# The first MoE's output projection taken out of the attention steps and made a phase of seven block products

## Chip, cores and metric

One NeuronCore of a Trainium2 chip. The metric is the device time of one execution in microseconds; a few runs are shown by their median. The engines are TensorE (PE, matrix products), VectorE (DVE), ScalarE (ACT), GpSimd (POOL) and SyncE (SP, which issues most DMA transfers).

## Reference

Attention with a causal mask and a decay bias, then two MoE layers that use all their weights for each token:

```python
scores = q @ k.T / 8 + min(bias(cumsum(max(s, 0))), 0)      # 4 batches, 8 heads, 576 tokens, 64 wide
x  = softmax(causal(scores)) @ v                            # 2304 tokens x 512
h  = max(max(x @ w1, x @ w2), x @ w3)                       # 512 -> 768
x2 = h @ w_out                                              # 768 -> 512, "first MoE's output projection"
h2 = (x2 @ w_a) * (x2 @ w_b)                                # 512 -> 1536
out = h2 @ w_out2                                           # 1536 -> 512
```

## The kernel before

**Products in two parts.** Each operand of a matrix product is kept as a rounded part "h" and a remainder "l" (a rounding on ACT or POOL, `rnd`, and a subtraction on DVE, `sub` or `hilo` at lines 937 to 939). A product takes three matmuls: h by h, h by l, l by h. The weights come as 64-bit numbers and are first made 32-bit (`conv_w`, line 234, and `to_f32`, line 915).

**Attention and first MoE.** The work is cut into eight steps: four batches, each with the first 256 tokens (R = 0) and the other 320 (R = 1). In a step four pairs of heads go through scores (PE), softmax (DVE, ACT, DVE, POOL), transposes (PE, copied by ACT) and the product with v (`f_pv`, line 520), whose result is split into Xh and Xl. The first three steps are "plain" (scores without the split). `moe1_units` (line 589) makes the first MoE's units of a step: 18 gate units of 12 matmuls (`gate`, line 594; ACT copies the first product into hf, DVE takes the two maxima, ACT rounds the result into hh and DVE writes hl), and four output units of 18 matmuls (`outp`, line 622; ACT copies the result into xo and its queue stores it to the DRAM tensor x2T, x transposed). The units of a step may start when all four pairs of that step are done. A list with positions (lines 805 to 874) spreads them over the next step's attention, with the attention at a higher priority; a list scheduler then fixes each engine's order, so that a unit's matmuls fill what the attention leaves free. The units that are left at the end run alone (lines 1092 to 1096), and between them pieces that prepare the second MoE are put in by hand, each after a "mark", the eviction of some unit.

**Second MoE.** Tokens are taken in three blocks of 768, and each 512-deep product of a block is made with seven products of half-size blocks instead of eight: `a_side` (line 942) and `b_side` (line 960) form seven operands from the four quarters with four sums each, and `Unit.prod` (line 1148) runs the products in the order 1, 2, 6, 5, 7, 4, 3 into three PSUM banks X, Y and Z. Products 6, 7 and 4 add onto bank X, which ACT copies after products 1, 6 and 7; product 3 adds onto Z. `x2_load` (line 1027, SP's queue) fetches x2T for a block, `x2_split` (line 1034) makes its operands. `w2_pieces` (line 990) prepares one of 12 column groups of both gate weights. `gates` (line 1179) is one unit of 7 x 6 matmuls of 384 columns. The results go to hT in DRAM, and a last phase of 256-column products makes the output.

**Memory.** Tiles lie in pools on a left and a right stack. A pool that is allocated with `reuse_waits="tile"` over released ones makes each new tile wait for the old tiles under it.

Of the kernel before, what the change touches and what calls it, by code (L numbers as in the profile page):

```python
# [29 lines left out]
def kernel(  # L30
# [18 lines left out]
    nc = tc.nc  # L49
# [56 lines left out]
    ap_ = tc.alloc_tile_pool(name="attn", bufs=1, side="right")  # L106

# [27 lines left out]
    x2T = dram.tile([DM, NT], F32, name="x2T")  # L135
# [117 lines left out]
    w1o = []  # L253
    w1_keys = [("g", g, m) for m in range(MF) for g in range(3)]
    w1_keys += [("o", m) for m in range(MF)]
    w1_t = {}

# [5 lines left out]
    NPRE = 4  # L263
    for p_, n0, n1 in zip(w1p, (0, 6, 11, 18), (6, 11, 18, NPRE - MF)):
        w1_tiles(p_, w1_keys[n0:n1])
# [30 lines left out]


# [7 lines left out]
    def load_pair(b, p, R):  # L305
# [9 lines left out]
        if b == 0 and p >= 2 and R == 0 and plain:  # L315
            t = mp.tile([P, MF * N1], F32, tag="hh" if bp == 2 else "hl", bufs=1, name="kqv")
# [260 lines left out]
    w1_pend = list(w1_keys)  # L577
# [11 lines left out]
    def moe1_units(R, b, X):  # L589
# [4 lines left out]
        def gate(m, g):  # L594
# [13 lines left out]
            if g == 0:  # L608
                st["h"] = mp.tile([P, N1], F32, tag="mt", bufs=2, name="hf")
                st["A"] = nc.scalar.copy(st["h"][:, :n], ps[:, :n])  # L610
            else:
                hf = st["h"][:, :n]
                st["V"] = nc.vector.tensor_tensor(hf, ps[:, :n], hf, op=ALU.max)  # L613
                mark(st["A"], st["V"])
            if g == 2:
                if m == 0:
                    st["hh"] = mp.tile([P, MF, N1], F32R, tag="hh", bufs=1, name="hh")
                    st["hl"] = mp.tile([P, MF, N1], F32R, tag="hl", bufs=1, name="hl")
                rnd("A", st["hh"][:, m, :n], hf)
                sub("V", st["hl"][:, m, :n], hf, f(st["hh"][:, m, :n]))  # L620

        def outp(c):
            ps = ps_m.tile([P, 512], F32, tag="m", name="o")
            hh, hl = st["hh"], st["hl"]
            mm = []
            for m in range(MF):
                key = ("o", m)
                if key not in w1h:
                    w1_need(key)
                mm += [(w1h[key], hh, m), (w1h[key], hl, m), (w1l[key], hh, m)]  # L630
            for i, (w, x, m) in enumerate(mm):
                nc.tensor.matmul(  # L632
                    ps[:, :n], w[:, c, :], x[:, m, :n],
                    start=(i == 0), stop=(i == len(mm) - 1),
                )
            xo = mp.tile([P, N1], F32, tag="mt", bufs=2, name="xo")
            mark(nc.scalar.copy(xo[:, :n], ps[:, :n]))  # L637
            nc.scalar.dma_start(x2T[c * P : (c + 1) * P, col : col + n], xo[:, :n])
# [6 lines left out]
        for c in range(KC):  # L645
            units.append((18 * w, lambda c=c: outp(c)))
# [217 lines left out]
    for j in range(MF):  # L864
        stream.append((W1 + (W2 - W1) * j / MF, 200, w_next))
# [9 lines left out]
    moe = [(1, m_next) for _ in range(len(todo))]  # L875
    ap_.release()

    TB = 384
    NSB = NT // (2 * TB)
    KH = KC // 2
    OPS = (1, 2, 6, 5, 7, 4, 3)
    sides = ("right", "left")

    rA = tc.alloc_tile_pool(name="rA", bufs=1, side="right", reuse_waits="tile")
    rA2 = tc.alloc_tile_pool(name="rA2", bufs=1, side="right", reuse_waits="tile")
    xr = {0: tc.alloc_tile_pool(name="xr0", bufs=1, side="right", reuse_waits="tile")}  # L900
    wpool = {0: rA}
    rawp = [rA2]
    nraw = [0]

    def load_raw(src):

        pool = rawp[nraw[0] % len(rawp)]
        nraw[0] += 1
        raw = pool.tile([P, WC, 2], I32, tag="raw", bufs=1, name="wraw")
        rv = raw.rearrange("p c t -> p (c t)")  # L910
        if not wide:
            return raw, nc.sync.dma_start(rv[:, :WC].bitcast(F32), src)
# [665 lines left out]
```

## Time and profile before

| | |
|---|---|
| runs, median (lowest, highest) | 906.07 us (906.06, 908.05), 3 runs |
| span of the profiled execution | 903.9 us, first to last instruction; the median is 2.2 us more |
| instructions | 17169 |
| TensorE clock granted | full in all 40 slices |
| busy share PE, DVE, ACT, POOL | 99%, 65%, 42%, 25% |
| HBM read, written | 77.29 MB, 23.94 MB |

The span starts with the attention; the last attention products end at 448 us, the last output unit of the first MoE at 498 us, the second MoE's gates at 757 us. Durations of matmuls in the profile overlap, so the pace of a stream of matmuls is read from a stretch divided by their count, not from their mean duration.

### The profile page before, as it was taken

What the parts mean: (1) busy time and instruction counts of PE and PEld (TensorE: products, weight loads), DVE (VectorE), ACT (ScalarE), POOL (GpSimd) and SP (SyncE); (2) the same over time, 40 slices, a digit from 0 to 9 for tenths busy, and PEclk for the clock granted to TensorE, in tenths of its full rate; (3) what the DMA queues carried; (4) which work ended last, traced back from release to release, by engine and by line L of the source; (5) the groups of instructions that cost most, each with busy time, mean ns of one, the idle gap of its engine ahead of it and who ended that gap; (6) DMA issues with size and microseconds to landing.
All of it is one profiled execution on the core that took longest, in us unless ns stands there. A gap on an engine that the chain in (4) does not pass through costs nothing.

```text
span 903.9 us, 17169 instructions
## 1 busy us (share of the span) xinstructions
PE 892.1 (99%) x6296; PEld 849.5 (94%) x6296; DVE 590.9 (65%) x1401; ACT 381.3 (42%) x877; POOL 223.8 (25%) x336
## 2 busy tenths in 40 slices
PE   7999999999999999999999999999999999999998
PEld 7677899999999999999999999999999999999998
DVE  4798543556545555455379567777675868997874
ACT  3656553656536565265433332223222223433321
POOL 6553421222312223132122102111111210321211
PEclk9999999999999999999999999999999999999999
DMA  5665441213322233221143214444443244254331
GB/s 180 218 197 189 128 118 30 88 48 104 99 62 73 62 103 91 70 60 51 45 156 131 85 48 154 158 155 146 146 146 123 99 157 141 80 168 157 99 117 47
DMA packets 57228, 102.36 MB, mean 113 GB/s; under 512 B 5960, under 2 KB 40680, under 8 KB 57144
## 3 DMA queue, kind: packets, MB, share of 16 engines
q1 hardware_dynamic: 52536, 96.54, 34.0%
q10 hardware_dynamic: 4608, 4.72, 1.6%
q8 instruction: 50, 0.82, 0.4%
q14 instruction: 34, 0.28, 0.1%
HBM read 77.29 MB, written 23.94 MB: 112 GB/s over the span
## 4 chain that ended last, share of the span: by engine, by line
PE 93%; DMA 3%; DVE 1%; issue 1%; SPq 1%; ACT 1%; POOL 0%; ACTq 0%; POOLq 0%
PE g L604 25%; PE X L1125 24%; PE Z L1125 12%; PE o L632 9%; PE Y L1125 6%; PE fpv L540 5%; PE t L556 3%; DMA wraw<-in_moe_w_dram 2%; PE f L473 2%; PE s L429 2%; PE s L430 2%; PE W L1125 1%; PE ft L515 1%; PE tj L569 1%; PE sj L463 1%
## 5 line engine op out<-in xcount | busy, mean ns | idle before, releaser
L604 PE MATMUL g<-Xh,hg 128*128 128x256 f32 (+1 forms) x576 | 174.4, 304 | 0.5 <-ACT xo L637 0.5
L604 PE MATMUL g<-Xh,lg 128*128 128x256 f32 (+1 forms) x576 | 172.8, 301 | 0.0
L604 PE MATMUL g<-Xl,hg 128*128 128x256 f32 (+1 forms) x576 | 172.5, 300 | 0.0
L604 PEld LDWEIGHTS g<-Xh,hg 128*128 128x128 f32 x576 | 108.5, 189 | 4.1 <-issue 2.0
L604 PEld LDWEIGHTS g<-Xl,hg 128*128 128x128 f32 x576 | 108.8, 189 | 2.3 <-issue 0.7
L604 PEld LDWEIGHTS g<-Xh,lg 128*128 128x128 f32 x576 | 108.7, 189 | 1.0 <-issue 0.8
L1125 PE MATMUL X<-xh,wh 128*128 128x384 f32 x288 | 97.3, 338 | 0.1
L1125 PE MATMUL X<-xl,wh 128*128 128x384 f32 x288 | 96.9, 336 | 0.0
L1125 PE MATMUL X<-xh,wl 128*128 128x384 f32 x288 | 96.9, 337 | 0.0
L88 POOL TENSOR_SCALAR wh<-wval 128x256 fp32r<-128x256 f32 x84 | 41.4, 502 | 181.8 <-DVE wval L929 134.7
L1125 PE MATMUL X<-woh,slot 128*128 128x256 f32 x408 | 76.6, 281 | 0.5 <-ACT ob L1168 0.5
L422 POOL TENSOR_SCALAR P<-P,rs 128x128 f32<-128x128 f32 (+2 forms) x80 | 51.8, 653 | 98.2 <-DVE rs L417 64.3
L935 DVE TENSOR_TENSOR slot<-hraw,slot 128x768 fp32r<-128x768 f32 x60 | 60.4, 1032 | 13.8 <-POOL slot L88 11.0
L935 DVE TENSOR_TENSOR u<-Z,u 128x384 f32<-128x384 f32 x72 | 39.7, 552 | 43.2 <-ACT u L1168 33.5
L613 DVE TENSOR_TENSOR hf<-g,hf 128x256 f32<-128x256 f32 (+1 forms) x96 | 43.5, 453 | 34.0 <-PE g L604 32.4
L1125 PEld LDWEIGHTS X<-woh,slot 128*128 128x128 f32 x408 | 64.3, 189 | 0.7 <-ACT ob L1168 0.7
L405 DVE CUSTOM_DVE_ANT_0 P<-s,maskJ 128x128 f32<-128x128 f32 (+2 forms) x80 | 40.3, 516 | 26.9 <-PE s L430 13.7
L632 PE MATMUL o<-hh,lo 128*128 128x256 f32 (+1 forms) x192 | 57.8, 305 | 0.0
L632 PE MATMUL o<-hh,ho 128*128 128x256 f32 (+1 forms) x192 | 57.0, 302 | 0.3 <-ACT xo L637 0.3
L1125 PE MATMUL X<-wol,slot 128*128 128x256 f32 x204 | 56.9, 280 | 0.0
L632 PE MATMUL o<-hl,ho 128*128 128x256 f32 (+1 forms) x192 | 56.5, 299 | 0.0
L412 ACT ACTIVATE P<-P,nm 128x128 f32<-128x128 f32 (+2 forms) x80 | 46.5, 582 | 22.6 <-DVE nm L405 16.9
(168 smaller groups left out, 2255.1 us busy)
## 6 DMA issues: line engine op xcount, KB each, us to landing
hT<-u SPq DMA_DIRECT2D x72, 192.0 KB
hraw<-hT SPq DMA_DIRECT2D x36, 384.0 KB
wraw<-in_moe_w_dram SPq DMA_DIRECT2D x18, 512.0 KB
wraw<-in_moe_w_out_dram SPq DMA_DIRECT2D x18, 512.0 KB
kraw<-in_kT_dram SPq DMA_DIRECT2D x24, 288.0 KB
wraw<-in_moe_w_a_dram SPq DMA_DIRECT2D x12, 512.0 KB
wraw<-in_moe_w_b_dram SPq DMA_DIRECT2D x12, 512.0 KB
out_dram<-ob SPq DMA_DIRECT2D x18, 256.0 KB
```

The lines of the kernel that those rows point to most:

```text
L88: nc.gpsimd.tensor_scalar(o, i, scale, 1.0, op0=ALU.mult, op1=ALU.mult)
L405: nc.vector.tensor_tensor_reduce(pt[:, c0 : c0 + w], v_, m_, -scale, first, op0=ALU.add, op1=ALU.min, accum_out=nm[:, i : i + 1],)
L412: e_ = nc.scalar.activation(pt[:, c0:c1], pt[:, c0:c1], AF.Exp, bias=first, scale=-1.0, accum_out=sm[:, g : g + 1],)
L422: nc.gpsimd.tensor_scalar(pt[:, c0:c1], pt[:, c0:c1], rs[:, g : g + 1], 1.0, op0=ALU.mult, op1=ALU.mult,)
L429: nc.tensor.matmul(ps, QA1[:, qs], KB1[:, h, ksl], start=True, stop=False)
L540: e_ = nc.tensor.matmul(ps[h * D : h * D + D, c0:n], w, x, start=(t == 0), stop=(t == len(mm[h]) - 1),)
L556: nc.tensor.transpose(ps[:, j * P : j * P + P], pt[:, j * P : j * P + P], ident)
L604: nc.tensor.matmul(ps[:, :n], w[:, kk, :], x[:, kk, :], start=(i == 0), stop=(i == len(mm) - 1),)
L613: st["V"] = nc.vector.tensor_tensor(hf, ps[:, :n], hf, op=ALU.max)
L632: nc.tensor.matmul(ps[:, :n], w[:, c, :], x[:, m, :n], start=(i == 0), stop=(i == len(mm) - 1),)
L935: return {"V": nc.vector, "P": nc.gpsimd}[e].tensor_tensor(o, a, b, op=op)
L1125: nc.tensor.matmul(ps[:, :n], w, x, start=(first and i == 0), stop=(i == len(mm) - 1), skip_group_check=not first,)
```

## The change

The output units leave `moe1_units`. A step's gate result hf is no longer split; ACT's queue stores it to a DRAM tensor h1T (768 x 2304). When all gate units are done, a new phase computes the projection for the three blocks of 768 tokens with the same seven products: the two halves of the 768 rows of h and of w_out are the inner halves, two units (p = 0, 1) give the 512 output columns. One product of one unit is 9 matmuls of 384 columns. The results stay in the SBUF tile xt (two blocks at a time), from which `x2_split` makes the second MoE's operands.

The weights of the projection are only made 32-bit and kept in the tiles vo, together with the first pair of second-MoE weights, which are now loaded in steps 1 and 2 and split at positions 2.2 and 2.4 of the list (`w20_side`). Their operands for the seven products are made behind the last attention step (`wo1_side`). Block 0's operands are made there too, in three slices, with sums on DVE and roundings shared between ACT and POOL. Blocks 1 and 2 use one tile hrB in turn: roundings on ACT, subtractions on DVE, sums on POOL, in six slots (A to F) that later products reuse. `chain` fixes PE's order in this phase.

```diff
-    w1p = [tc.alloc_tile_pool(name=f"w1p{i}", bufs=1, side="left") for i in range(4)]
+    w1p = [tc.alloc_tile_pool(name=f"w1p{i}", bufs=1, side="left") for i in range(3)]
...
+    rA = tc.alloc_tile_pool(name="rA", bufs=1, side="right")
+    vo = tc.alloc_tile_pool(name="vo", bufs=1, side="right")
...
-    x2T = dram.tile([DM, NT], F32, name="x2T")
+    h1T = dram.tile([MF * P, NT], F32, name="h1T")
...
+    side_keys = [("o", m) for m in range(MF)] + [("c", 0), ("c", 1)]
...
+    def load_side(key, raw):
+
+        while len(side_v) < 2:
+            side_v.append(vo_tile(f"vo{len(side_v)}"))
+        if key[0] == "o":
+            h, k = divmod(key[1], MF // 2)
+            to_f32(raw, [(side_v[h][:, k * WC : (k + 1) * WC], slice(0, WC))])
+        else:
+            o = [t[:, KM * WC :].rearrange("r (s c) -> r s c", s=2)[:, key[1]] for t in side_v]
+            to_f32(raw, [(o[0], slice(0, 2 * P)), (o[1], slice(2 * P, 4 * P))])
...
             if g == 0:
-                st["h"] = mp.tile([P, N1], F32, tag="mt", bufs=2, name="hf")
+                st["h"] = mp.tile([P, N1], F32, tag="mt", bufs=4, name="hf")
...
             if g == 2:
-                if m == 0:
-                    st["hh"] = mp.tile([P, MF, N1], F32R, tag="hh", bufs=1, name="hh")
-                    st["hl"] = mp.tile([P, MF, N1], F32R, tag="hl", bufs=1, name="hl")
-                rnd("A", st["hh"][:, m, :n], hf)
-                sub("V", st["hl"][:, m, :n], hf, f(st["hh"][:, m, :n]))
-
-        def outp(c):
...
-            nc.scalar.dma_start(x2T[c * P : (c + 1) * P, col : col + n], xo[:, :n])
+                nc.scalar.dma_start(h1T[m * P : (m + 1) * P, col : col + n], hf)
...
-        for c in range(KC):
-            units.append((18 * w, lambda c=c: outp(c)))
...
-    for j in range(MF):
-        stream.append((W1 + (W2 - W1) * j / MF, 200, w_next))
+    ns = len(side_keys)
+    for j in range(ns):
+        stream.append((W1 + (W2 - W1) * j / ns, 200, w_next))
+    for j in range(2):
+        stream.append((W2 + 0.2 * (j + 1), 200, lambda j=j: w20_side(j)))
...
+    def h_load(sb, k0, k1, q):
 
         t0 = 2 * sb * TB
+        for n in (0, 3, 1, 2):
+            k, t = n % 2 * KM, t0 + n // 2 * TB
+            nc.sync.dma_start(q[:, n], h1v[:, k + k0 : k + k1, t : t + TB])
...
+    pieces = {
+        0: lambda: (h_fetch(0), h_fetch(1)),
+        1: lambda: h_split(0, hq[0], EN, (0,), 0, 1),
+        2: lambda: h_split(0, hq[0], EN, (1,), 0, 1),
+        3: lambda: h_fetch(2),
+        4: lambda: h_split(0, hq[1], EN, (0,), 1, 2),
+        5: lambda: h_split(0, hq[1], EN, (1,), 1, 2),
+        7: lambda: h_split(0, hq[2], EN, (0,), 2, 3),
+        8: lambda: h_split(0, hq[2], EN, (1,), 2, 3),
+    }
...
+    with tc.high_priority(300):
+        after(marks[-13], lambda: wo1_side(0, (0,)))
+        after(marks[-12], lambda: wo1_side(1, (0,)))
+        after(marks[-10], lambda: wo1_side(0, (1,)))
+        after(marks[-9], lambda: wo1_side(1, (1,)))
...
+    def oproj(p, sb):
+
+        o = xt[:, sb % 2, p]
...
+            for k in range(KM):
+                out_ += [
+                    (wh[:, k], xh[:, k]), (wh[:, k], xl[:, k]), (wl[:, k], xh[:, k]),
+                ]
...
+        return Unit(
+            TB, mms, lambda: o[:, 0], lambda: o[:, 1], lambda: o[:, 3],
+            lambda ps, t: nc.scalar.copy(o[:, 2], ps), lambda t: None,
+        )
+
+    def h_op(sb, i, n):
+        hilo(HE[i], hop[sb][0][i], hop[sb][1][i], hq[sb][:, n])
+
+    def h_sum(sb, o, a, b, op):
+        q = hq[sb]
+        tt("P", q[:, o], q[:, a], q[:, b], op)
+
+    HE = dict(zip((1, 2, 4, 6, 5, 7, 3), "AAAAAAA"))
+
+    def h_sums(sb):
+        h_sum(sb, 3, 2, 3, ALU.add)
+        h_sum(sb, 2, 0, 2, ALU.subtract)
+        h_sum(sb, 0, 3, 0, ALU.subtract)
+        h_sum(sb, 1, 1, 0, ALU.subtract)
+
+    def run_sb(sb, plan):
+        us = [oproj(p, sb) for p in range(2)]
+        for n, i in enumerate(OPS):
+            for u in us:
+                u.prod(i)
+            for fn in plan.get(i, ()):
+                fn()
+
+    SLOT = {
+        1: {1: "A", 2: "B", 4: "C", 6: "D", 5: "E", 7: "F", 3: "B"},
+        2: {1: "A", 2: "D", 4: "E", 6: "F", 5: "C", 7: "B", 3: "D"},
+    }
+    SRC = {1: 0, 2: 1, 4: 3, 6: 0, 5: 3, 7: 2, 3: 1}
...
+    def h_make(sb, i):
+        s_ = SLOT[sb][i]
+        h_tile(slots1[s_], sb, i, s_)
+        h_op(sb, i, SRC[i])
+
+    def x0_split(k, part):
+        q = [xt[:, 0, k : k + 1, n] for n in range(4)]
+        behind(lambda: x2_split(0, k, k + 1, q, EN, (part,)))
...
+    hq[1] = hq[2] = hrB.tile([P, 4, KM, TB], F32, name="hrB")
+    with tc.high_priority(300):
+        h_load(1, 0, KM, hq[1])
+    run_sb(0, {
+        1: [lambda: h_make(1, 1), lambda: h_make(1, 4)],
+        2: [lambda: h_make(1, 2), lambda: h_sums(1)],
+    })
+    hs0.release()
+    vo.release()
...
+    with tc.high_priority(100):
+        h_make(1, 6)
+        h_make(1, 5)
+        h_make(1, 7)
+        for n in (0, 3, 2):
+            h_load1(2, n)
...
+    run_sb(1, {
+        1: [lambda: h_make(2, 1), lambda: x0_split(0, 0)],
+        2: [lambda: h_make(1, 3), lambda: h_load1(2, 1), lambda: x0_split(0, 1)],
+        6: [lambda: h_make(2, 2)],
+        5: [lambda: h_make(2, 4), lambda: h_sums(2)],
+        7: [lambda: h_make(2, 6), lambda: x0_split(1, 0), lambda: more_raw(1)],
+        4: [lambda: h_make(2, 5), lambda: x0_split(1, 1)],
+        3: [lambda: h_make(2, 7)],
+    })
+    run_sb(2, {2: [lambda: h_make(2, 3)]})
...
+    with tc.high_priority(100):
+        after(hist[-4], lambda: q1[0](0, wa))
+        more_raw(1)
+        after(hist[-3], lambda: q1[0](1, wb))
+        after(hist[-2], lambda: q1[1]((0,)))
+        after(hist[-2], lambda: q1[1]((1,)))
+        after(hist[-2], lambda: xt_split(1, (0,)))
+        after(hist[-1], lambda: xt_split(1, (1,)))
```

## Rows read from the trace of the kernel before

**Rows 1.** The page: engines' busy time over the span; granted TensorE clock by slice.

```profile
PE 892.1 (99%) x6296; PEld 849.5 (94%) x6296; DVE 590.9 (65%) x1401; ACT 381.3 (42%) x877; POOL 223.8 (25%) x336
...
PEclk9999999999999999999999999999999999999999
```

**Rows 2.** PE's waits: engine, line <- releaser: us in total, times, longest.

```profile
PE f L473 <- DMA kqv<-in_kq_dram: 3.6, 1, 3.6
...
PE t L556 <- POOL F L422: 0.2, 1, 0.2
```

**Rows 3.** The page: the chain that ended last, share of the span by line.

```profile
PE g L604 25%; PE X L1125 24%; PE Z L1125 12%; PE o L632 9%; PE Y L1125 6%; PE fpv L540 5%; PE t L556 3%; DMA wraw<-in_moe_w_dram 2%; PE f L473 2%; PE s L429 2%; PE s L430 2%; PE W L1125 1%; PE ft L515 1%; PE tj L569 1%; PE sj L463 1%
```

**Rows 4.** Windows: us, each engine's busy us (instructions), granted clock, DMA share, GB/s.

```profile
core 0: us, PE busy (x) PEld busy (x) DVE busy (x) ACT busy (x) POOL busy (x), PEclk, DMA share, GB/s
45.00:100.00 55.00, 54.81 (x375) 40.71 (x375) 47.34 (x137) 31.88 (x77) 25.18 (x32) 1.00 0.57 178
90.00:120.00 30.00, 30.00 (x221) 25.00 (x217) 15.89 (x67) 18.63 (x57) 11.89 (x19) 1.00 0.41 121
186.60:300.40 113.80, 113.80 (x887) 108.29 (x886) 60.62 (x195) 62.05 (x158) 29.80 (x48) 1.00 0.28 79
457.00:487.00 30.00, 30.00 (x205) 30.00 (x205) 28.46 (x63) 12.60 (x26) 9.56 (x16) 1.00 0.51 171
560.00:757.00 197.00, 196.90 (x1131) 196.58 (x1130) 142.16 (x303) 58.97 (x114) 31.59 (x62) 1.00 0.43 142
```

**Rows 5.** The chain in order of time: start, us, what (two unbroken pieces).

```profile
101.96 1.68 PE o L632 x14
...
161.55 2.20 PE o L632 x15
```

**Rows 6.** Groups by line: out<-in xcount | busy us, mean ns | idle before.

```profile
L92 DVE TENSOR_TENSOR hl<-hf,hh 128x256 fp32r<-128x256 f32 (+1 forms) x48 | 23.9, 498 | 7.4 <-ACT hh L81 7.4
L81 ACT ACTIVATE hh<-hf 128x256 fp32r<-128x256 f32 (+1 forms) x48 | 21.2, 441 | 35.7 <-DVE hf L613 35.6
...
L637 ACT COPY xo<-o 128x256 f32<-128x256 f32 (+1 forms) x32 | 12.4, 396 | 15.1 <-PE o L632 12.4 <-DMA x2T<-xo 2.6
```

**Rows 7.** Instructions on x2T: xcount: ns min/median/max, first and last start.

```profile
L638 ACTq DMA_DIRECT2D x2T<-xo x32: 326/326/443, 108.2 to 499.0; - x32
L1032 SPq DMA_DIRECT2D xt<-x2T x16: 338/424/469, 446.0 to 502.2; - x16
```

**Rows 8.** Timeline of DVE, back to back: start us, us, what.

```profile
460.20 0.55 DVE L935 TENSOR_TENSOR xl<-xt,xh 128x384 fp32r<-128x384 f32 x1
460.67 0.55 DVE L935 TENSOR_TENSOR xt<-xt 128x384 f32<-128x384 f32 x1
461.13 0.48 DVE L613 TENSOR_TENSOR hf<-g,hf 128x320 f32<-128x320 f32 x1
...
512.45 0.95 DVE L935 TENSOR_TENSOR xl<-xt,xh 128x768 fp32r<-128x768 f32 x1
513.31 0.55 DVE L935 TENSOR_TENSOR u<-Z,u 128x384 f32<-128x384 f32 x1
```

**Rows 9.** Groups by line and shape, columns as in rows 6.

```profile
L935 DVE TENSOR_TENSOR wl<-wval,wh 128x256 fp32r<-128x256 f32 x84 | 35.4, 435 | 0.3 <-POOL wh L88 0.3
...
L81 ACT ACTIVATE xh<-xt 128x768 fp32r<-128x768 f32 x10 | 7.9, 843 | 1.1 <-DVE xt L935 1.1
...
L88 POOL TENSOR_SCALAR xh<-xt 128x384 fp32r<-128x384 f32 x6 | 4.5, 751 | 25.0 <-DVE xt L935 12.7 <-DMA xt<-x2T 12.3
...
L81 ACT ACTIVATE xh<-xt 128x384 fp32r<-128x384 f32 x8 | 4.1, 528 | 7.5 <-DMA xt<-x2T 4.0 <-DVE xt L935 3.5
...
L182 POOL TENSOR_TENSOR cl<-cs,ch 16x1152 fp32r<-16x1152 f32 x1 | 2.6, 2620 | 0.3 <-ACT ch L181 0.3
```

**Rows 10.** Timeline of POOL behind the attention.

```profile
459.36 0.52 POOL L88 TENSOR_SCALAR xh<-xt 128x384 fp32r<-128x384 f32 x1 [5.60 <-DVE xt L935]
463.63 1.76 POOL L88 TENSOR_SCALAR xh<-xt 128x384 fp32r<-128x384 f32 x1 [3.76 <-DVE xt L935]
```

**Rows 11.** DMA from 457 to 487 us in 40 slices, GB/s.

```profile
GB/s 0 266 83 0 0 0 0 0 0 0 0 109 186 377 99 221 369 381 295 287 326 348 385 309 148 229 355 393 355 93 11 0 0 0 0 0 153 333 353 358
```

More of the change, by code (lines that the diff above doesn't have):

```diff
@@ new lines, in to_f32 @@
+    def to_f32(raw, outs):
+        if not wide:
+            rv = raw.rearrange("p c t -> p (c t)")[:, :WC].bitcast(F32)
+            for o, c in outs:
+                nc.vector.tensor_copy(o, rv[:, c])
+            return
+        L = raw[:, :, 0]
+        Hw = raw[:, :, 1]
+        nc.scalar.activation(
+            f(Hw), f(Hw), AF.Prelu, scale=2.0 ** -112, alpha=-(2.0 ** 32)
+        )
+        nc.vector.tensor_scalar(L, L, 29, None, op0=ALU.logical_shift_right)
+        for o, c in outs:
+            nc.vector.scalar_tensor_tensor(
+                o.bitcast(I32), Hw[:, c], 3, L[:, c],
+                op0=ALU.logical_shift_left, op1=ALU.bitwise_or,
+            )
@@ new lines, in b_side, with w2_ops @@
+    def b_side(q, sp, part):
+        b11, b12, b21, b22 = q
+        if 0 in part:
+            sp(1, b11)
+            sp(2, b21)
+            sp(3, b22)
+            tt("V", b11, b12, b11, ALU.subtract)
+            tt("V", b12, b22, b12, ALU.subtract)
+            tt("V", b22, b22, b11, ALU.subtract)
+            tt("V", b21, b21, b22, ALU.subtract)
+        if 1 in part:
+            sp(6, b22)
+            sp(5, b11)
+            sp(7, b12)
+            sp(4, b21)
+    def w2_ops(pool, c):
+        hi, lo = {}, {}
+        for i in OPS:
+            for d, x in ((hi, "h"), (lo, "l")):
+                d[i] = pool.tile(
+                    [P, 2 * P], F32R, tag=f"w{x}{i}", bufs=1, name=f"w{x}{i}_{c % 2}"
+                )
+        wm[c] = hi, lo
+        return hi, lo
@@ new lines, with load_raw, more_raw @@
+    wpool = {0: rA}
+    rawp = [rA2]
+    nraw = [0]
+    def load_raw(src):
+        pool = rawp[nraw[0] % len(rawp)]
+        nraw[0] += 1
+        raw = pool.tile([P, WC, 2], I32, tag="raw", bufs=1, name="wraw")
+        rv = raw.rearrange("p c t -> p (c t)")
+        if not wide:
+            return raw, nc.sync.dma_start(rv[:, :WC].bitcast(F32), src)
+        return raw, nc.sync.dma_start(rv, src.bitcast(I32))
+    raws = []
+    coming = []
+    def more_raw(n):
+        for src in coming[:n]:
+            raws.append(load_raw(src))
+        del coming[:n]
+        return raws[-1][1].ins
@@ new lines, in load_w2, with x2_split, sp @@
+    def load_w2(c):
+        conv, side = w2_pieces(c)
+        for n, src in enumerate((wa, wb)):
+            conv(n, src)
+        if coming:
+            more_raw(2)
+        side((0, 1))
+    xs = {}
+    def x2_split(sb, k0, k1, q, eng, part):
+        if sb not in xs:
+            xs[sb] = {}, {}
+            for i in (1, 2, 4, 6, 5, 7, 3):
+                pool = xr1[{1: 0, 2: 0, 4: 1, 6: 1}.get(i, 2)] if sb == 1 else xr[sb]
+                for d, c in zip(xs[sb], "hl"):
+                    d[i] = pool.tile([P, KH, TB], F32R, name=f"x{c}{sb}{i}")
+        hi, lo = xs[sb]
+        es = dict(zip((1, 2, 4, 6, 5, 7, 3), eng))
+        def sp(i, src):
+            hilo(es[i], hi[i][:, k0:k1], lo[i][:, k0:k1], src)
+        a_side(q, sp, part)
@@ L1177 @@
+    strict[0] = False
+    hs1b.release()
+    hs1a.release()
+    hs1A.release()
+    hrB.release()
+    for p_ in reversed(wops):
+        p_.release()
+    rawB = lpool("rawB")
+    wpool[1] = lpool("wB")
+    xr1 = [lpool(f"xr1{n}") for n in range(3)]
+    tmpA = lpool("tmpA")
+    xr[2] = lpool("xr2")
+    wo32 = []
     hT = dram.tile([MF2 * P, NT], F32, name="hT")
@@ L1292 @@
     tmpA.release()
-    xr1b.release()
-    xr[1].release()
+    for p_ in reversed(xr1):
+        p_.release()
     wpool[1].release()
```

373 lines of the change are left out of this document (148 added, 225 removed).

## Prediction

> **What bounds the kernel now.** I read the page first: TensorE (PE) is busy for 892.1 of 903.9 us at full granted clock (2.4 GHz) in every slice, VectorE (DVE) is second with 590.9 us [rows 1]. Then PE's waits: the longest is 3.6 us, at the start, and a transpose that waited for POOL's normalised softmax is the only wait inside the attention, 0.2 us [rows 2]. So the kernel is as long as PE's instruction stream, and an edit counts by what it does to that stream or by an idle stretch that it opens. The chain of waits, followed back from the end, gives the output projection ("o L632") 9% of the span on the page [rows 3]. The windows show how near the next engine is: DVE is 86% busy in 45 to 100 us, 53% in a batch of the steady attention (186.6 to 300.4 us), 95% in the gate units behind the last attention step (457 to 487 us), and PE has no gap beside it even there [rows 4].
>
> **PE's work.** Before: four units of 18 matmuls in each of eight steps, 288 matmuls of 256 columns and 288 of 320. In unbroken pieces of the chain 14 of the first kind take 1.68 us (120 ns each), 15 of the second 2.20 us (147 ns) [rows 5]: 34.6 + 42.3 = 76.9 us. After: 3 blocks x 2 units x 7 products x 9 matmuls = 378 of 384 columns. The second MoE's gates are that shape; 1131 of them fill 196.9 us [rows 4], 174 ns each: 65.8 us. The step is worth 11.1 us.
>
> The rows give columns / 2.4 plus some 13 ns. The Trainium skill ("TensorE: Matmul & The Clock Gate", Back-to-back issue gap) gives an isolated gap of columns / 2.4 plus 2.5 ns. By it the same count would be 70.6 us before and 61.4 us after, so 9.2 us instead of 11.1; the trace does not agree and decides.
>
> **What leaves the attention.** With each unit's rounding and subtraction of hh and hl (48 + 48 instructions, 21.2 us of ACT, 23.9 of DVE) and the 32 evictions xo (12.4 us ACT) [rows 6], no PE time goes, since PE waited for none of them. The round trip of x2T also goes; no wait on it stands among PE's, so it is worth 0. In its place ACT issues 48 stores of hf instead of 32 of xo, 0.33 us each [rows 7]: 16 x 0.33 = 5.2 us in 450 us, on a queue 55% busy. Each store waits on ACT for DVE's maximum, as the rounding that it replaces did, so nothing new queues behind it; hf has four buffers instead of two. SP's queue loses 16 loads of x2T [rows 7] and gains 20 of h1T. The weights of the projection and the first pair of second-MoE weights are converted in steps 1 and 2: cover is the PE stream there; if that fails they cost DVE 3 to 4 us.
>
> **The attention without its fill.** This is the term the trace does not show. Of the 576 matmuls all but step 7's 72 now stand among attention instructions, 66 us of fill. In a steady batch PE would have 113.8 - 72 x 0.120 - 72 x 0.147 = 94.6 us; ACT keeps 62.1 - (21.2 + 12.4)/4 = 53.7 us (57%), DVE 60.6 - 23.9/4 = 54.6 us (58%) [rows 4, 6]. Both stay under the 86% at which PE still ran without gaps, so by throughput the cost is 0. By latency it is open: the only row is the 0.2 us wait, and 0.2 us for each of the 24 later pairs would be 4.8 us. The early place is 90 to 120 us: step 0's projection (72 x 0.120 = 8.6 us) is nearly the only fill while the last plain pairs of step 1 run, because step 1's own gates need all of its pairs. ACT is busy 18.6 us of those 30 [rows 4] and would have to fit into 21.4. Bounds there 0 and 8.6 us. A reason excludes a gain: PE is full now. I take 1.5 us for both places, near the zero end, as ACT and DVE have room.
>
> **The phase: preparing block 0.** Behind the last attention step PE has 18 gate units, 216 x 0.147 = 31.7 us. DVE has there 21 subtractions and 12 sums for block 0 and 14 + 8 for the weights, all of 128x384 and 0.47 us apart back to back [rows 8], 25.9 us, and 12 maxima of 0.48 [rows 8], in all 31.6 us. That is full, but the operands of products 4 and 3 are not wanted for another 15.7 us. Cost 0, upper bound 2 us.
>
> **Blocks 1 and 2.** One block takes PE 22.0 us, one product (two units) 3.14. A half-operand of 128x1152 costs ACT 1.16 us and DVE 1.25 (estimates, from 0.47 and 0.86 us for DVE at 384 and 768 columns [rows 8], and 0.53 and 0.84 for ACT [rows 9]). DVE in block 1: 7 x 1.25, 22 instructions for x of block 0 and 6 evictions at 0.47, 21.9 of 22.0 us; in block 0 only 10.3; what slips has the third block as cover. The four sums per block go to POOL. Its only two-input row is 2.62 us for the same 1152 columns on 16 partitions [rows 9]. Beside a busy DVE POOL is slower: copies of 128x384 mostly take 0.51 us, one 1.76, on average 0.75 [rows 9, 10]. So a sum costs 2.62 to 9.0 us; by the mean's factor (1.47) I take s = 3.85.
>
> Block 1: its load (2.36 MB) waits for the X tiles of the last gate, so it starts with block 0. The busiest slices behind the attention move some 355 GB/s [rows 11]: 6.6 us; with issue and landing I take 9. Three sums and one half-operand later (9 + 3s + 2.4 = 23) product 6 is wanted at 28.3. Covered. Block 2: product 4's half-operand takes the slot of block 1's product 5, free at 22.0 + 12.6, so the sums start at 37.0; product 6 has its operand at 37.0 + 11.6 + 2.4 = 51.0 and is wanted at 44.0 + 6.3 = 50.3. Wait 0.7 us, from 0 to 16.
>
> Product 4 adds onto the bank that ACT copies after product 7, one unit (1.57 us) earlier: 0.48 us of copy behind a 1.16 us rounding is 1.64. At 0.07 for six units, and something for the semaphores, 0.5 us (0 to 2). The second MoE's third unit needs block 1's x, its second the second pair of weights. Their preparation may start when the first unit's product 7 of the last block is done, 7.9 us before the second MoE, and is for DVE 11 instructions of 0.86 us and 11 of 0.44 (the weights' subtractions [rows 9]), 14.3 us, of which the weights are wanted 15.2 and x 22.5 us after that start: 0.5 us (0 to 3).
>
> **Sum.** -11.1 + 1.5 + 0.7 + 0.5 + 0.5 = -7.9 us on the profiled execution, 903.9 to 896.0 of span. The median of the runs is 906.07, 2.2 us above that span for what lies around it; I forecast **898.2 us**. A measurement of this kernel can tell about 0.3% (2.7 us) from no change.
>
> **Rivals.** *All covered.* The waits stay at zero, as before; for it speaks that the kernel has none now, even with DVE at 95%. 906.07 - 11.1 = 895.0.
>
> *POOL's sums are locked out (slower).* One POOL copy at 1.76 us shows the mechanism; against it, the mean is 0.75. Waits: block 1 11.4 + 3s - 28.3, block 2 3s + 39.4 - 50.3. At s = 7.5 they are 5.6 and 11.6 us, together 17.2, and the time 906.07 - 11.1 + 2.5 + 17.2 = 914.7. It eats the gain from s = 6.0 and is slower by 0.3% from s = 6.5, 2.5 times the row.
> The Trainium skill ("SBUF — State Buffer", Who interferes with whom) says that a DVE instruction with two SBUF inputs contends with a GpSimd instruction that reads SBUF, and the subtractions are such; no row here shows a 128-partition sum beside them.
>
> *The fill was needed.* The stretch from 90 to 120 us keeps its length: 8.6 instead of 1.5 us, 905.3; for it speaks a chain over four engines per pair and that the gates of step 1 cannot come earlier, against it ACT's and DVE's room. If later pairs wait 0.2 us each as well, 910.
>
> **Chances.** Forecast (896.5 to 902) 0.46; all covered 0.24; fill 0.18, of which 0.03 faster, 0.10 same, 0.05 slower; POOL 0.09; other slower outcomes 0.03. So faster 0.73, same 0.10, slower 0.17. The range goes from 894 (all covered, less 1 us for what the pitches are rounded by) to 909, which takes in the fill rival and leaves out POOL's. The likeliest sign's own range is 894 to 903.
>
> **What would show it.** Right: "o L632" absent, a stretch of 378 matmuls at 174 ns behind the gates, steady batches of about 95 us, PE's waits a few us in total with POOL or ACT as releaser at products 6 and 4. POOL sums near 3.9 us. Wrong: PE waits for DVE or POOL in every attention pair, an idle stretch between 90 and 120 us, a wait over 3 us at product 6, or a phase much over 70 us. The forecast falls if the matmul pitch of the phase is not that of the gates.

## The result and the profile after

The kernel after takes 916.36 us (median of 4 runs, 914.74 to 917.58) against 906.07 before; the ratio is 1.0114, 95% interval 1.0092 to 1.0136. It is slower by some 10 us. The forecast was 898.2, and the range ended at 909. A trace shows one execution, and the granted clock differs from one to the next: its mean over the span is 0.987 to 0.993 in the four executions of the kernel after, and 0.998 in the traced one of the kernel before against 0.996 in most of its others.

The profiled execution of the kernel after has a span of 915.4 us, 11.5 more than before. Its page, engines and granted clock by slice, beside [rows 1]:

```profile
PE 888.1 (97%) x6098; PEld 841.3 (92%) x6098; DVE 627.9 (69%) x1436; ACT 383.2 (42%) x847; POOL 257.1 (28%) x361
...
PEclk8999999999999999999998999999999999999999
```

PE has 198 matmuls less, as worked out, and is busy for 4.0 us less, but the span is longer: PE now waits. The waits of PE, in the form of [rows 2] (us in total, times, longest):

```profile
PE X L1077 <- DVE hl L339: 4.8, 1, 4.8
PE f L576 <- DMA kqv<-in_kq_dram: 4.4, 1, 4.4
PE Z L1077 <- DVE xt L339: 2.8, 1, 2.8
...
PE g L707 <- DVE hf L716: 1.9, 3, 0.9
PE X L1077 <- ACT xt L1118: 1.4, 1, 1.4
PE f L576 <- DVE nm L508: 1.3, 2, 0.9
PE f L576 <- DMA kraw<-ck: 1.1, 2, 0.9
PE X L1077 <- ACT hh L81: 0.8, 1, 0.8
PE X L1077 <- ACT xt L1124: 0.8, 1, 0.8
PE t L659 <- POOL F L525: 0.8, 1, 0.8
```

Line 1077 is the matmul of `chain`, so five of these stand in the new phase, 10.7 us together, and "g" is a gate unit behind the last attention step. The waits on "nm" (DVE's maximum of the scores), "ck" (the rows written over a key tile) and "F" (POOL's normalised softmax) all stand between 80 and 120 us, in the early attention; from 120 us to the end of the attention PE waits for nothing.

**Where the time went.** One instruction serves as the mark, because both kernels execute it at the same point of the work: a product with v of step 3 (`fpv`, 320 columns). PE's timeline of the kernel before:

```profile
186.54 2.28 PE L540 MATMUL fpv<-PF,qvraw 128*64 128x320 f32 x20
```

and of the kernel after, with the same place one batch later:

```profile
174.53 2.27 PE L643 MATMUL fpv<-PF,qvraw 128*64 128x320 f32 x20
...
269.09 2.28 PE L643 MATMUL fpv<-PF,qvraw 128*64 128x320 f32 x20
```

Up to the mark 144 output matmuls are gone, 72 x 0.120 + 72 x 0.147 = 19.2 us by [rows 5], and of gate matmuls as many stand ahead of it as before (523 and 520 recorded), but the mark comes only 12.0 us earlier: 7.2 us are lost. From there on nothing is: the next batch takes 94.56 us. The windows (us, each engine's busy time with its count, granted clock, DMA share, GB/s) of the kernel before in the early stretch:

```profile
0.00:45.00 45.00, 38.10 (x228) 30.18 (x229) 28.13 (x94) 22.32 (x62) 26.66 (x43) 0.96 0.64 200
...
45.00:95.00 50.00, 49.81 (x339) 37.56 (x339) 43.59 (x126) 29.97 (x73) 23.44 (x30) 1.00 0.59 185
95.00:120.00 25.00, 25.00 (x189) 21.23 (x188) 12.70 (x54) 15.44 (x49) 9.62 (x16) 1.00 0.43 124
```

and of the kernel after, also for the steady batch, the tail of gate units and the last part of the phase:

```profile
0.00:45.00 45.00, 38.18 (x225) 30.40 (x226) 27.82 (x94) 22.07 (x60) 26.55 (x42) 0.92 0.66 200
45.00:95.00 50.00, 48.44 (x329) 36.13 (x328) 39.60 (x114) 28.34 (x67) 19.20 (x25) 1.00 0.69 230
95.00:120.00 25.00, 22.75 (x140) 16.28 (x139) 16.50 (x68) 14.29 (x42) 10.95 (x19) 0.93 0.30 92
...
174.53:269.09 94.56, 94.56 (x740) 89.08 (x739) 54.46 (x184) 55.20 (x140) 28.28 (x48) 1.00 0.37 108
...
396.00:430.00 34.00, 32.10 (x217) 31.30 (x214) 32.99 (x63) 8.47 (x19) 16.43 (x21) 1.00 0.13 43
...
476.00:507.00 31.00, 23.84 (x120) 23.26 (x121) 23.31 (x32) 9.56 (x15) 11.39 (x8) 0.89 0.14 52
```

The 7.2 us are idle time of PE from 45 to 120 us (1.56 + 2.25 against 0.19 before, 3.6 us), a granted clock of 0.93 in the last 25 of them (1.75 us) and one of 0.92 instead of 0.96 in the first 45 (1.8 us). The last of these is not shown to belong to the change: the trace of o_cut4, which runs the kernel before up to there, has 0.87 in the first 45 us, and of two traces whose program is the same there late_dve has 0.96 and order26 0.92. Without it 5.4 us are lost. How the rest divides between idle time and clock differs by execution too: sums_dve, with the same program up to the mark, reaches it at 174.80 us with 5.6 us of idle time and the full clock from 45 to 120 us. In the tail the 18 gate units take 33.6 instead of 31.7 us, with DVE busy for 32.99 of 34.

In the phase the pitch is the forecast one: at the full clock the matmuls start 174 ns apart (18 of them from 479.22 to 482.34 us). What it loses stands in PE's timeline:

```profile
477.55 0.45 PE L1077 MATMUL Z<-hh,who 128*128 128x384 f32 x1 [2.82 <-DVE xt L339]
477.83 0.34 PE L1077 MATMUL Z<-hl,who 128*128 128x384 f32 x1
478.01 0.33 PE L1077 MATMUL Z<-hh,wlo 128*128 128x384 f32 x1
...
486.44 0.44 PE L1077 MATMUL X<-hh,who 128*128 128x384 f32 x1 [0.81 <-ACT hh L81]
491.68 0.69 PE L1077 MATMUL X<-hl,who 128*128 128x384 f32 x1 [4.80 <-DVE hl L339]
492.17 0.52 PE L1077 MATMUL X<-hh,wlo 128*128 128x384 f32 x1
492.49 0.52 PE L1077 MATMUL X<-hh,who 128*128 128x384 f32 x1
```

Block 1's product 3 waits 2.82 us for an eviction (the copy or sum that empties a PSUM bank), block 2's product 6 waits 0.81 + 4.80 for its operand, and behind that wait the matmuls start 320 ns apart until 497 us: the granted clock has fallen to its lower level (1.2 GHz), which costs some 2.5 us over 18 of them. The account is -11.1 (count and pitch) + 7.2 (early stretch) + 1.9 (tail) + 10.7 (waits of the phase) + 2.5 (clock) = +11.2, against the 11.5 measured between the two traces; without the 1.8 us of the first 45 it is 9.4, and the medians lie 10.3 apart.

**DVE is what is late in blocks 1 and 2.** Its timeline:

```profile
470.65 2.65 DVE L324 TENSOR_SCALAR wraw<-wraw 128x512 int32<-128x512 int32 x1
473.22 3.81 DVE L339 TENSOR_TENSOR hl<-hrB,hh 128x1152 fp32r<-128x1152 f32 x1
...
477.42 2.54 DVE L339 TENSOR_TENSOR xl<-xt,xh 128x384 fp32r<-128x384 f32 x1
...
484.55 3.00 DVE L339 TENSOR_TENSOR xt<-xt 128x384 f32<-128x384 f32 x1
...
490.28 1.35 DVE L339 TENSOR_TENSOR hl<-hrB,hh 128x1152 fp32r<-128x1152 f32 x1
```

The subtraction that product 6 waited for is the last row. Four instructions ahead of it take 2 to 2.5 us more than their like, and each began while a sum on POOL ran (the sums begin at 470.35, 473.09, 475.89 and 484.27 us). The eviction that product 3 waited for stood behind the 3.81 us.

### The profile page after: what moved, and what is told of

Its sections match the earlier page's. It is cut to its first block, busy times and chain, and to the rows that moved or that the text cites. A ratio compares the mean times of both kernels' runs of the same rounds, so it can differ in the third digit from the quotient of the medians.

```text
span 915.4 us, 16842 instructions
## 1 busy us (share of the span) xinstructions
PE 888.1 (97%) x6098; PEld 841.3 (92%) x6098; DVE 627.9 (69%) x1436; ACT 383.2 (42%) x847; POOL 257.1 (28%) x361
## 4 chain that ended last, share of the span: by engine, by line
PE 81%; DMA 7%; DVE 6%; issue 2%; POOL 1%; SPq 1%; ACT 1%; ACTq 0%; POOLq 0%; DVEq 0%
PE X L1077 26%; PE g L707 20%; PE Z L1077 13%; PE Y L1077 7%; PE fpv L643 5%; PE t L659 2%; DVE hl L339 2%; PE s L532 2%; PE s L533 1%; PE f L576 1%; DMA kraw<-in_kq_dram 1%; DMA wraw<-in_moe_w_dram 1%; PE ft L618 1%; POOL hrB L339 1%; DMA wraw<-in_moe_w_out_dram 1%
## 5 line engine op out<-in xcount | busy, mean ns | idle before, releaser
L88 POOL TENSOR_SCALAR wh<-wval 128x256 fp32r<-128x256 f32 x77 | 38.6, 510 | 180.0 <-DVE wval L326 126.1
L525 POOL TENSOR_SCALAR P<-P,rs 128x128 f32<-128x128 f32 (+2 forms) x80 | 47.4, 598 | 100.3 <-DVE rs L520 72.8
L508 DVE CUSTOM_DVE_ANT_0 P<-s,maskJ 128x128 f32<-128x128 f32 (+2 forms) x80 | 40.8, 515 | 21.6 <-PE s L533 11.1
L1077 PEld LDWEIGHTS X<-xh,wh 128*128 128x128 f32 x288 | 54.1, 188 | 0.5 <-DVE u L339 0.3
L1077 PEld LDWEIGHTS X<-xl,wh 128*128 128x128 f32 x288 | 54.1, 188 | 0.0
L1077 PEld LDWEIGHTS X<-xh,wl 128*128 128x128 f32 x288 | 54.0, 188 | 0.0
```

Source lines behind the costliest of these rows:

```text
L88: nc.gpsimd.tensor_scalar(o, i, scale, 1.0, op0=ALU.mult, op1=ALU.mult)
L508: nc.vector.tensor_tensor_reduce(pt[:, c0 : c0 + w], v_, m_, -scale, first, op0=ALU.add, op1=ALU.min, accum_out=nm[:, i : i + 1],)
L525: nc.gpsimd.tensor_scalar(pt[:, c0:c1], pt[:, c0:c1], rs[:, g : g + 1], 1.0, op0=ALU.mult, op1=ALU.mult,)
L1077: e_ = nc.tensor.matmul(ps[:, :n], w, x, start=(first and i == 0), stop=(i == len(mm) - 1), skip_group_check=not first,)
```

## The experiments

All ratios are to the kernel before, timed on the same chip beside each run (medians of 905.80 to 906.40 us in the experiments). "The kernel after" is the base of each edit unless another is named.

| run | median us | ratio, 95% interval |
|---|---|---|
| after | 916.36 | 1.0114, 1.0092 to 1.0136 |
| sums_dve | 913.44 | 1.0069, 1.0050 to 1.0087 |
| late_side | 914.38 | 1.0085, 1.0060 to 1.0111 |
| late_dve | 912.15 | 1.0054, 1.0037 to 1.0070 |
| o_cut0 | 902.62 | 0.9957, 0.9945 to 0.9970 |
| o_cut4 | 897.62 | 0.9919, 0.9899 to 0.9938 |
| fill_back | 921.77 | 1.0173, 1.0156 to 1.0190 |
| order26 | 910.78 | 1.0063, 1.0043 to 1.0083 |
| order26_act | 906.97 | 1.0010, 0.9998 to 1.0022 |
| s1_own | 901.52 | 0.9949, 0.9936 to 0.9962 |
| kq_ahead | 899.45 | 0.9932, 0.9917 to 0.9947 |

### The four sums on DVE (sums_dve)

```diff
-        tt("P", q[:, o], q[:, a], q[:, b], op)
+        tt("V", q[:, o], q[:, a], q[:, b], op)
```

> The four operand sums of blocks 1 and 2 run on DVE instead of POOL. Theory A (a POOL sum of 2.7 us holds the DVE instruction that meets it, four DVE instructions of the last blocks took 2.2 us longer than their kind): DVE gets 8 x 1.25 = 10 us more work but loses the stretched instructions, the waits of 4.8 and 2.8 us in front of products 6 and 3 fall under 1.5 us each and the half-speed stretch behind the longer one goes; 916.4 falls to 906 to 910 us. Rival B (DVE has simply too much work in blocks 1 and 2): the added 10 us stand on the path, the waits grow, 918 to 924 us.

Groups by line and shape from 430 to 500 us in the kernel after (columns as in rows 6):

```profile
L339 POOL TENSOR_TENSOR hrB<-hrB 128x1152 f32<-128x1152 f32 x8 | 23.6, 2951 | 14.7 <-DVE xt L339 12.3 <-DVE hl L339 1.9
...
L339 DVE TENSOR_TENSOR hl<-hrB,hh 128x1152 fp32r<-128x1152 f32 x14 | 21.2, 1526 | 6.7 <-ACT hh L81 6.7
L339 DVE TENSOR_TENSOR xl<-xt,xh 128x384 fp32r<-128x384 f32 x14 | 10.0, 727 | 1.9 <-POOL xh L88 1.9
L339 DVE TENSOR_TENSOR xt<-xt 128x384 f32<-128x384 f32 x8 | 6.8, 856 | 0.0
...
L324 DVE TENSOR_SCALAR wraw<-wraw 128x512 int32<-128x512 int32 x2 | 3.1, 1538 | 0.0
```

and with the sums on DVE:

```profile
L339 DVE TENSOR_TENSOR hl<-hrB,hh 128x1152 fp32r<-128x1152 f32 x14 | 19.3, 1387 | 6.3 <-ACT hh L81 6.3
L339 DVE TENSOR_TENSOR hrB<-hrB 128x1152 f32<-128x1152 f32 x8 | 10.8, 1353 | 0.1
L339 DVE TENSOR_TENSOR xl<-xt,xh 128x384 fp32r<-128x384 f32 x14 | 7.7, 562 | 0.8 <-POOL xh L88 0.8
...
L339 DVE TENSOR_TENSOR xt<-xt 128x384 f32<-128x384 f32 x8 | 4.4, 546 | 0.0
...
L324 DVE TENSOR_SCALAR wraw<-wraw 128x512 int32<-128x512 int32 x2 | 0.8, 418 | 0.0
```

The four groups lose 1.9 + 2.3 + 2.4 + 2.3 = 8.9 us when POOL has no sums. So the sums in their POOL form took 8.9 us of DVE's time anyway, of the 10.8 us that they cost DVE when it does them itself: moving them to POOL had freed 2 us of DVE, not 10.8. The Trainium skill ("SBUF — State Buffer", Who interferes with whom) says that whoever issues first holds the shared ports for its whole instruction and the other stands still. The rows agree: DVE was mostly the one that stood still, and POOL's sums (median 2.71 us) stayed near the 2.62 us of [rows 9]; two sums that began while a subtraction of 128x1152 was going (at 442.51 and 475.89 us) took 3.62 and 3.66. The time falls by some 3 us, which is less than theory A's range and far from rival B's. Waits of 1.0 and 2.3 us in block 2 are left, and a stretch at the lower clock behind them, so contention was a part of the cause and not all.

### Weights of the phase prepared later, alone and with the sums on DVE (late_side, late_dve)

```diff
-        stream.append((W1 + (W2 - W1) * j / ns, 200, w_next))
+        stream.append((3.2 + 1.6 * j / ns, 200, w_next))
...
-        stream.append((W2 + 0.2 * (j + 1), 200, lambda j=j: w20_side(j)))
+        stream.append((5.2 + 0.4 * (j + 1), 200, lambda j=j: w20_side(j)))
```

> The eight side weights (six of the projection, two of the second MoE) are loaded and converted in list positions 3.2 to 4.8 instead of 1.3 to 1.8, their operands at 5.6 and 6.0 instead of 2.2 and 2.4; the phase is unchanged. Theory F (the first steps lost the output units as PE's fill, 7 us, and it is the chain of the softmax that sets their length): at most 1.5 us faster, 915 to 917 us. Rival L (loads and conversions of the side weights on SP, DVE and ACT hold the first steps up): 4 to 7 us faster, 909.5 to 912.5 us.

> Both edits together. The two places lie 300 us apart, so the gains should add: under A with L 899 to 906 us, under A with F 905 to 910 us, under B with F 917 to 924 us.

The time is lower by 2.0 us with late_side alone, and late_dve is 1.3 below sums_dve; neither theory's range of late_side holds 914.38, and F's is the nearer. The mark, at 174.53 and 174.80 us in the two traces with the early weights, lies at 171.42 in late_side, 172.96 in late_dve, and 170.86 to 173.58 in the three later traces whose program is theirs up to there (mean of the five 172.2). The loads and conversions that the change puts into steps 1 and 2 (DMA share 0.69 instead of 0.59 from 45 to 95 us) are thus some 2 us of the early loss, and most of it has another cause. The 912.15 us of late_dve lie in none of its three ranges, and the wait of product 6 that is left there (2.3 us) shows a second cause. Its rounding on ACT was ready at 481.1 us, but DVE, which takes its instructions in the order that the scheduler wrote down, first made the fourth sum, which only product 3 needs, two pieces for x, an eviction and a weight conversion, and began the subtraction at 484.71.

### Output matmuls cut from the kernel before (o_cut0, o_cut4), and fill put back (fill_back)

```diff
             # before, line 631, in outp
+            if b == 0 and R == 0:      # o_cut4: b == 2
+                mm = mm[:1]
```

> The kernel before, with 17 of 18 matmuls left out in each of the four output units of step 0 (first 256 tokens of batch 0); evictions, stores, weights and all loads stay. PE work falls by 68 x 0.120 = 8.2 us. Theory F (this work was fill that the first steps needed): at most 4 us of it are gained, 902 to 906 us. Rival L (fill was not needed there, the side weights cost the time in the changed kernel): 7 to 8.2 us are gained, 898 to 899 us.

> Control for the cut in step 0: the kernel before with 17 of 18 matmuls left out in each of the four output units of step 4 (first 256 tokens of batch 2), in the steady attention. Theory F: there nothing waits for fill, all 8.2 us are gained, 898 to 899 us. If the attention needs fill everywhere: at most 4 us, 902 to 906 us.

> The changed kernel with four units of 17 matmuls of 256 columns put back at the end of step 0's list, where the output units stood; they read a gate weight and Xh and nothing reads their result (68 x 0.120 = 8.2 us of PE work added). Theory F (PE has idle time there since the fill is gone): at most 4 us of it are paid, 916 to 920.5 us. Rival L (PE has no idle time to give there): 923.5 to 925 us.

The same 8.2 us of matmuls are taken out of the kernel before at two places. Out of step 4 all of it is gained (8.2 us by the medians, ratio 0.9919). Out of step 0 about half is (3.8 us, 0.9957), and the window of that run shows the rest as idle PE (4.2 us), where the kernel before had none:

```profile
95.00:120.00 25.00, 20.76 (x139) 15.93 (x140) 13.75 (x61) 17.05 (x54) 9.22 (x17) 1.00 0.42 130
```

Put back into step 0 of the kernel after as matmuls that nobody reads, 8.2 us cost 5.4 by the medians, between the ranges of the two theories: about a third is absorbed. So with everything else of the change absent the early stretch already needs about half of step 0's fill, and step 4, in the steady batches, none of its own. This is the forecast's term "attention without its fill": 4.4 us of these 8.2, where it took 1.5.

### Block 2's product 6 moved up (order26), and the tail's roundings to ACT (order26_act)

On late_dve: block 2's operand for product 6 gets a higher priority, and the fourth sum, product 3's operand and a weight conversion come behind it. order26_act also moves POOL's roundings of the tail to ACT.

```diff
+    def h_make26():
+        with tc.high_priority(400):
+            m26.append(h_make(2, 6).ins)
...
+    def late_sum():
+        with tc.issue_after(m26[0]):
+            h_sum(2, 1, 1, 0, ALU.subtract)
+            h_make(2, 3)
...
-        after(hist[-3], lambda: q1[0](1, wb))
+        after(hist[-2], lambda: q1[0](1, wb))
...
+    EA = "AAAAAAA"
...
-        1: lambda: h_split(0, hq[0], EN, (0,), 0, 1),
+        1: lambda: h_split(0, hq[0], EA, (0,), 0, 1),
...
-            lambda i, q: hilo("P", hi[i], lo[i], q), part,
+            lambda i, q: hilo("A", hi[i], lo[i], q), part,
```

> As the kernel with late side weights and DVE sums (912.2 us), but in DVE's order the subtraction for block 2's product 6 stands ahead of the fourth sum and of two second-MoE weight instructions, which come later. Theory S (block 2 waits because DVE's fixed order puts 3.6 us of later work between the ready rounding and this subtraction, and the wait costs more behind it since TensorE then runs at half clock for some 28 matmuls, about 4 us): the wait of 2.3 us falls under 1 us, the half-clock stretch shrinks or goes, 905 to 909 us. Rival B (DVE is overfull from block 1 on, so the order doesn't matter): the wait moves to another product, 911 to 913 us.

> As order26, and behind the last attention step all roundings for block 0 and for the projection's weights run on ACT instead of POOL. Theory A (a POOL instruction that reads SBUF holds the DVE subtraction that meets it, here 0.78 to 0.85 instead of 0.47 us): DVE's work there shrinks by some 4 us and the 2.2 us in which gate units wait for DVE's maxima go, 1.5 to 2.5 us less than order26. If DVE's stretched instructions have another cause, no change (within 0.7 us).

In order26 the wait for product 6's operand falls from 2.3 to 0.4 us, and no gain is shown (ratio 1.0063 after 1.0054): the other unit's product 6, which in late_dve waited 1.0 us for a copy on ACT right behind it, now waits 3.6. The run with the roundings on ACT is at the time of the kernel before (1.0010). It is 3.8 us below order26, where 1.5 to 2.5 were forecast; the gate units' 1.9 us are gone, and so is a wait of 1.2 us for a copy on ACT in block 0, but the other unit's product 6 still waits for its copy, now 4.6. DVE's, ACT's and PE's timelines there:

```profile
483.05 1.41 DVE L339 TENSOR_TENSOR xl<-xt,xh 128x384 fp32r<-128x384 f32 x2 [0.40 <-POOL xh L88]
...
484.49 0.48 ACT L1119 COPY xt<-X 128x384 f32<-128x384 f32 x1 [2.45 <-DVE xl L339]
...
485.02 0.48 PE L1078 MATMUL X<-hh,who 128*128 128x384 f32 x1 [4.58 <-ACT xt L1119]
```

The copy is that of block 2's product 1, made long before. It goes into the buffer of xt that holds block 0's x, and has to wait until the last split of that x has read it; product 6 adds onto the bank that the copy empties. This chain lay behind the late operand, and where the operand came earlier PE met it instead.

### A tile of its own for that copy (s1_own)

```diff
+    s1p = rpool("s1p")
+    own = s1p.tile([P, 2, TB], F32, name="own")
     rA2 = rpool("rA2")
...
-            TB, mms, lambda: o[:, 0], lambda: o[:, 1], lambda: o[:, 3],
+            TB, mms, lambda: own[:, p] if sb == 2 else o[:, 0], lambda: o[:, 1], lambda: o[:, 3],
...
+        if sb == 2:
+            q[0] = own
```

> Edit: as the run before (all splits behind the attention on ACT, sums on DVE, block 2's product 6 moved up), and product 1 of block 2 is copied into a small tile of its own instead of xt's first quarter, which block 0's x split still reads. Theory (what is left of the phase's loss is a chain of reuse: product 6 of block 2 waits for a copy that waits for that split, and the idle time then costs a stretch at half clock): the 4.6 us wait and the stretch of 3.5 us at half clock behind it go, PE's waits between 430 and 500 us stay under 1.5 us in total, and the span falls by 5 to 8 us: 899 to 902 us, ratio 0.992 to 0.996; what then separates it from the 898.2 of the prediction is the early stretch. Rival (DVE is simply full in blocks 1 and 2, and the wait moves to the next instruction that is late): another wait of 3 us or more on DVE or ACT appears at a later product or at the second MoE's first units, 905 us or more, ratio over 0.998.

901.52 us, ratio 0.9949: faster than the kernel before, and within the theory's range. The 4.6 us wait is gone; 0.66 us are left for a bank that the second MoE's first unit needs, and 0.85 at block 2's product 6. The lower clock is not quite gone; PE's timeline:

```profile
478.04 0.41 PE L1078 MATMUL Y<-xh,wh 128*128 128x384 f32 x1 [0.66 <-DVE own L339]
...
480.17 0.50 PE L1078 MATMUL X<-hl,who 128*128 128x384 f32 x1 [0.85 <-DVE hl L339]
480.47 0.52 PE L1078 MATMUL X<-hh,wlo 128*128 128x384 f32 x1
```

The matmuls start 320 ns apart from 480.5 to 483.7 us. What separates this run from the forecast is mostly the early stretch, whose chain of waits (start, us, what) now reads:

```profile
102.44 3.75 DMA kraw<-in_kq_dram
...
106.80 1.86 DMA kraw<-ck
...
108.79 1.62 PE f L576 x4
```

A key tile comes free when the scores of an earlier pair have read it, the next pair's keys are loaded into it, and two of its rows are then written over by further transfers: 6.2 us with PE at the end of it. The kernel before issues the same transfers at 101.33 and 105.12 us and ran output matmuls meanwhile [rows 5].

### Key loads of step 2 into unused buffers (kq_ahead)

On s1_own. The two tiles vo lie unused in step 2 there, since the weights come later.

```diff
-        if b == 0 and p >= 2 and R == 0 and plain:
+        if R == 0 and plain and (b, p) in ((0, 2), (0, 3), (1, 0), (1, 1)):
             t = vo_tile("kqv")[:, : MF * N1]
...
-            nc.sync.dma_start(kt_[0:66, : 4 * nk], kq0[bp])
+            with tc.issue_after(last_ld[-1]) if b == 1 else nullcontext():
+                nc.sync.dma_start(kt_[0:66, : 4 * nk], kq0[bp])
...
```

> Edit: the run before (901.5 us), and the keys of the first two pairs of step 2 are loaded into the two 8 KB buffers that lie unused there, in the same place of SP's queue, instead of the two key buffers whose earlier content must first be used up by the scores of step 1; nothing else changes. Theory (what PE waits for between 95 and 120 us, once the fill is gone, is a round trip of DMA for each pair: the key buffer comes free, the load of 3.8 us, then 1.9 us for the row that is written over it): PE's wait on kraw<-ck (1.7 us) and the half-clock stretch at 110 to 115 us (2.1 us lost) go, the last attention step ends 2.5 to 4 us earlier than 395 us, and the time is 897.5 to 899.5 us, ratio to before 0.991 to 0.993. Rival (the chain of a pair over the engines, from scores over maximum, exponent, sum and normalisation to the transposes, needs the fill, as the forecast's rival had it): PE waits as long, on POOL, DVE or ACT instead, the end of the attention moves by less than 1 us, and the time stays at 900.5 to 902.5 us.

899.45 us, ratio 0.9932. The wait on the keys ("kraw<-ck", 1.2 to 1.7 us in the five traces with late weights) is gone, and a wait of 0.9 us for DVE's maximum appears. In PE's timeline the product at 110 us is still slow; behind it the mark, and block 2's product 6 in the phase:

```profile
110.28 3.58 PE L645 MATMUL fpv<-PF,qvraw 128*64 128x320 f32 x20
...
172.10 2.27 PE L645 MATMUL fpv<-PF,qvraw 128*64 128x320 f32 x20
...
479.71 0.44 PE L1080 MATMUL X<-hl,who 128*128 128x384 f32 x1 [0.85 <-DVE hl L339]
```

The median is 2.1 us lower than s1_own's, but the two intervals against before overlap, and the trace does not show the gain: the last attention product comes at 391.46 us, 1.8 us earlier than in s1_own's trace (393.30), yet in the other four traces with late weights, where the keys are loaded as in s1_own, it comes at 390.61 to 392.67, and the mark, at 172.10, lies at the mean of all five (172.2). So the transfers are what PE waits for in s1_own; that this wait sets the length of the stretch is not shown, and behind it the chain of the engines (keys, scores, maximum, exponent, normalisation) holds PE next, as the rival had it. This version has the lowest median: 0.7% under the kernel before.

## Why the prediction was wrong

**Right.** The count and the pitch: 174 ns per matmul of 384 columns and -11.1 us. The steady batch without its fill, forecast at 94.6, took 94.56 us, and none of the later pairs waited. The instructions of ACT and DVE and the stores that left the attention brought nothing, as forecast: the steady batch fell by its matmuls alone. PE did not wait for the load of block 1. Three of the signs named for being wrong appeared: idle time between 90 and 120 us, a wait over 3 us at product 6, and a phase well over 70 us (65.8 and 13.2 us of waits and clock).

**The attention without its fill** was forecast at 1.5 us; 7.2 were lost in the early stretch, 5.4 without the clock of the first 45 us. Some 2 of them belong to the weights in steps 1 and 2 (late_side), which were priced at nothing because "cover is the PE stream there"; that stream had lost its fill. The bounds 0 to 8.6 held the loss; the choice "near the zero end, as ACT and DVE have room" is the step that failed. Busy shares say nothing of a chain in which each engine works once and the next waits. A reading failed with it: the 0.2 us wait was taken for the only one inside the attention, but the same table of the kernel before has, at 37 us, where an early pair runs,

```profile
PE f L473 <- DVE nm L405: 1.0, 1, 1.0
```

that is, scores waiting for DVE's maximum. o_cut0 shows that about half of step 0's fill is needed, and o_cut4 that the steady step needs none. Which links of the early chain set its length is not shown: the key tile's reuse with its transfers is one that PE waits for (s1_own), and with it gone the gain is not clear of the scatter (kq_ahead). The rival "the fill was needed" had the mechanism, with a chance of 0.18.

**Blocks 1 and 2** were forecast at 0.7 us. Block 2's product 6 waited 5.6 us for its operand, and 2.5 more went to the clock. The failed step is "21.9 of 22.0 us; what slips has the third block as cover". What slipped was not needed last: product 6 of block 2 is the third product of that block, and its operand stood in DVE's queue behind work that is needed later (late_dve), after POOL's sums had held DVE up (sums_dve). Its bank stood behind a copy that a third block's use of xt held up (order26), a reuse that the forecast never listed. So order26 alone gained nothing that shows, and the three edits from late_dve to s1_own, one of which also ended the gate units' wait, gained some 10 us (ratio 1.0054 to 0.9949).

**POOL's sums** were forecast at 3.85 us and took 2.95 on average, so the duration was over-, not underestimated. The failed step was to look for the price on POOL: DVE paid it, 8.9 us of held instructions (sums_dve). The rival "locked out" gave 914.7 us, near the result, but by sums of 7.5 us that do not occur; that its number is near says nothing for it.

**Evictions** (0.5 us, 0 to 2) were mis-sized: 5.1 us. Block 1's product 4, the place that the forecast named, waited 0.81 us for its copy; block 0's product 6 waited 1.42 for another copy on ACT, and block 1's product 3 2.82 for an eviction on DVE behind a held subtraction. **Preparing block 0** was put at 0 with an upper bound of 2, and cost 1.9: its 31.6 us of DVE were counted at 0.47 us each, but beside a rounding on POOL the subtractions follow each other 0.78 us apart. With the roundings on ACT the wait goes (order26_act). **The clock** had no term in the sum at all; waits were priced at their own length only, and the page's digits, all 9 before, had hidden the 0.96 of the first 45 us.

What stays open: which links of the early chain set its length and what shortening them would give, and what decides whether the clock falls behind a given wait.

## What to carry to other kernels

Work that fills PE between the links of a chain is worth only what the chain does not need: before taking it out, follow one pair through its transfers and engines in the stretch with the least other fill, and price the stretch by that chain's length, not by busy shares. When an engine is planned at 99% with "cover later", list what each product waits for in the order in which that engine will take it, and the tiles that are reused; late things hide behind each other, and a single fix can show nothing until the last of them is gone. An instruction moved to POOL to relieve DVE relieves it only if DVE's instructions beside it are not held up.

## Not expected of the hardware

A DVE instruction that meets a two-input sum of 128x1152 on POOL is held for most of that sum: 0.42 to 2.65 us, 0.55 to 2.54 and 3.00, 1.35 to 3.81, while the sums take 2.95 on average. One of the held instructions (L324) has a single input. An eviction beside the same sums, which reads one input from PSUM, was not held: 0.55 us at 476.95, 0.56 at 446.00 and 447.56.

The length of a gap did not by itself decide whether the clock fell. Behind 2.82 us of idle PE (477.55 us in the kernel after) the matmuls went on at 174 ns; behind 0.81 and 4.80 us with one matmul between them they went on at 320 ns; and in s1_own they did so behind 0.66 and 0.85 us with six matmuls between. In kq_ahead the same two matmuls waited 0.65 and 0.85 us, again with six matmuls between, and the matmuls went on at 174 to 180 ns, so the same short waits can cost the clock in one execution and not in another.
